# An attention and MoE kernel: the low parts of the second pair's K and V are made a step later, and four pieces of bias rows go through another pool

## Chip, cores and metric

The kernel runs on one core of a Trainium2 chip. The metric is device time of one execution in microseconds (us); lower is better. A kernel is timed in several executions, and the median is quoted.

## What is computed

The first half is attention over 4 batches, 8 heads, 576 positions and 64 features, with a bias on the scores that a small network makes from the positions. The second half takes each token's 512 attention outputs through two weight matrices with a squared ReLU between them.

```python
scores = (1.0 / np.sqrt(D)) * np.matmul(q, k.transpose(0, 1, 3, 2))
rel = pos[:, None] - pos[None, :]
x = (np.log1p(np.abs(rel)) / np.log1p(np.maximum(pos[:, None], 1.0)))[..., None]
bias = np.maximum(x @ w1 + b1, 0.0) @ w2           # 32 hidden, one value a head
scores = scores + bias.transpose(2, 0, 1)[None, :, :, :]
attn = softmax(scores)                             # over the last axis
attn_out = np.matmul(attn, v)
x = attn_out.transpose(0, 2, 1, 3).reshape(B * S, H * D)    # 2304 x 512
h = np.maximum(x @ w_in, 0.0)                      # 512 -> 2048
out = (h * h) @ w_out                              # 2048 -> 512
```

Inputs and output are float32. The kernel keeps that precision with fp16 matmuls by splitting each operand into a high part (the value cast to fp16) and a low part (the value minus its high part, again fp16), and by adding up the products high x high, high x low and low x high.

## The kernel before

**Tiling.** The four batches are packed into two pairs, p = 0 and 1. The 576 query positions of a pair are cut into five chunks c: c = 0 holds the last 64 positions of both batches, c = 1 to 4 hold 128 positions of each of the two batches. A step is one chunk and one head, so a pair has 40 steps and the program 80 (t = 0 to 79). The second pair begins at step 40, and all five chunks of a pair use the same K and V of a head.

**One step.** `qk` makes the scores in PSUM (L413 to L425). `softmax_a` adds the bias rows `bt` and takes the row maximum on VectorE (L441, two instructions for a chunk of two batches, with a short one each that reads the maximum out), then ScalarE takes exp into `s` (L445, L447). `softmax_b` casts `s` to the high part of `a` on ScalarE (L129), GpSimd subtracts for the low part (L473, L474), and a DMA on SyncE's queue transposes `a` to `at` (L476). `pv` multiplies by V three steps later (LAG = 3, L506). After four heads VectorE scales the result into `x` (L518), and after eight `finish_x` splits and transposes the finished block (L535 to L546), which then waits in a queue for the second half of the program.

**MoE units.** That half is cut into units of 256 hidden columns, and about one unit runs in each step between the attention's matmuls. `g1` makes `hp` (L560), ScalarE takes the ReLU into `r` (L566), VectorE squares it (L568) and casts the high part of `g` (L133), GpSimd subtracts for its low part (L570). `g2` follows two units later and adds to the output `o` in PSUM (L583); after eight units ScalarE evicts `o` to SBUF (L590), and it is written out (L593).

**K and V of the second pair** are read, split and laid down while the first pair still runs. A load on SyncE's queue brings one head's K or V into a staging buffer `stg` (L179; three buffers). Then `KV.split` issues, in this order: the high part as a cast on GpSimd (L131), the low part on VectorE (L191 for K, L156 for V), for V a fill of one block of the low part with zeros on GpSimd (L160), and for K a copy of one corner to the tile `kz` on ScalarE (L196, two instructions). One such split is issued at the end of each step from 32 to 35, two in steps 36 to 39, one in steps 40 to 43; each is followed by the load of a later piece. The staging buffers serve the two weight matrices before.

**Bias rows.** `hgen` makes the hidden layer for a group of rows, `bias_mm` multiplies it on TensorE (L348), evicts the sums to a tile `be` (L369 on ScalarE, or VectorE) and writes that to a DRAM table `biasd` (L378), from which `bt` is read for each step (L394). `be` takes a buffer of the `r` pool, which has five and is shared with `r`, with `o` and with the casts `cv` of the weights; of the first 16 evictions every second takes one of the four buffers of the `g` pool.

**What sets the order.** The function emits the steps one by one. A scheduler then simulates the program and fixes for each engine one order of instructions, by priorities that follow the emission and are shifted for some kinds of work. On the chip each engine, and SyncE's queue too, runs its row in order: what stands behind a waiting instruction waits as well. `pinned()` and `behind()` add dependencies that only order instructions of the same engine.

Of the kernel before, what the change touches and what calls it, by code (L numbers as in the profile page):

```python
# [12 lines left out]
AF = mybir.ActivationFunctionType  # L13
ALU = mybir.AluOpType
# [6 lines left out]
QS, KS, VS = 7, 0, 9  # L21
# [24 lines left out]
NKZ = 8  # L46
# [5 lines left out]
def tile_attention_moe(  # L52
# [11 lines left out]
    nc = tc.nc  # L64
# [49 lines left out]
    kz = const.tile([128, NKZ, 2, 128], F16, name="kz")  # L114
# [5 lines left out]
    now = [0]  # L120

    def zn(key, i=None):
        v = ENG[key]
        i = now[0] // 8 if i is None else i
        return v[min(i, len(v) - 1)]

    def cast(eng, out, in_, scale=1.0):
        if eng == "A":
            nc.scalar.activation(out=out, in_=in_, func=AF.Copy, scale=scale)  # L129
        elif eng == "P":  # L130
            nc.gpsimd.tensor_scalar(out, in_, scale, 1.0, op0=ALU.mult, op1=ALU.mult)  # L131
        else:
            nc.vector.tensor_scalar(out, in_, scale, None, op0=ALU.mult)  # L133
# [9 lines left out]
    k_t, v_t, q_t, v32 = {}, {}, {}, {}  # L143
    f32c = [(0, c) for c in ORDER[0][:NF]]

    def as_f32(t):
        return t.rearrange("p a b -> p (a b)").bitcast(F32)

    def v_split(p, h, st):
        t = vp.tile([128, 2, 640], F16, tag="v", name="v")  # L150
        cast(zn("vh", p * 8 + h), t[:, 0, :], st, float(2 ** VS))
        if p == 0:
            cast("P", st, st, float(2 ** VS))
            nc.gpsimd.tensor_tensor(t[:, 1, :], st, t[:, 0, :], op=ALU.subtract)
        else:
            nc.vector.scalar_tensor_tensor(  # L156
                out=t[:, 1, :], in0=st, scalar=float(2 ** VS), in1=t[:, 0, :],
                op0=ALU.mult, op1=ALU.subtract)

        nc.gpsimd.memset(t[64:128, 1, :].rearrange("p (b j) -> p b j", b=2)[:, :, 256:320], 0.0)  # L160
        v_t[p, h] = t

    class KV:
        def __init__(self, p, h, which):
# [16 lines left out]
        def split(self):  # L181
            st = self.st
            if self.which == "k":
                n = self.p * 8 + self.h
                t = kp.tile([128, 2, S], F16, tag="k", name="k")
                st = st[:, 0:S]
                cast(zn("kh", n), t[:, 0, :], st, float(2 ** KS))
                if zn("kl", n) == "P":
                    nc.gpsimd.tensor_tensor(t[:, 1, :], st, t[:, 0, :], op=ALU.subtract)
                else:  # L190
                    nc.vector.scalar_tensor_tensor(  # L191
                        out=t[:, 1, :], in0=st, scalar=float(2 ** KS), in1=t[:, 0, :],
                        op0=ALU.mult, op1=ALU.subtract)
                for b in range(2):
                    r = slice(64 * b, 64 * b + 64)
                    nc.scalar.activation(out=kz[r, n % NKZ, :, r], in_=t[r, :, 512 - 512 * b:576 - 512 * b], func=AF.Copy)  # L196
                k_t[self.p, self.h] = t
            elif self.p:
                v_split(self.p, self.h, st[:, 0:640])
# [75 lines left out]
    nbe = [0]  # L275

    def hg_z(G):
        return int(HID[groups.index(G) // 2])
# [4 lines left out]
    def dlen(G):  # L283
        return max(S - 16 * G, 16 * G + 16)
# [51 lines left out]
    def bias_mm(G, gi):  # L336
        ts_ = hg.pop(G)
        z = hg_z(G)
        D_ = dlen(G)
        F_, M_ = S - 16 * G, 16 * G + 16  # L340
        cuts = [0, D_] if D_ <= 512 else [0, 288, D_]
        for d0, d1 in zip(cuts[:-1], cuts[1:]):
            if gi < 4 and d0:
                bp = ps_o.tile([128, 512], F32, tag=f"o{gi % 2}", name="bp")
            else:
                bp = ps_h.tile([128, 512], F32, tag="h", name="bp")
            for t in range(4):
                nc.tensor.matmul(out=bp[32 * t:32 * t + 32, 0:d1 - d0],  # L348
                                 lhsT=w2s if gi < 4 or PATS[z][t] == "A" else w2n,
                                 rhs=ts_[t][:, d0:d1],  # L350
                                 start=True, stop=True, tile_position=(0, 32 * t))

            parts = [(max(d0, 1), min(d1, M_), True), (d0, min(d1, F_), False)]
            parts = [x for x in parts if x[1] > x[0]]
            runs = [parts] if d0 == 0 and sum(e - a for a, e, _ in parts) <= 512 else [[x] for x in parts]
            for run in runs:
                nbe[0] += 1
                if nbe[0] <= 16 and nbe[0] % 2:

                    be = as_f32(g_p.tile([128, 2, 512], F16, tag="g", name="be"))  # L360
                else:
                    be = r_p.tile([128, 512], F32, tag="r", name="be")
                p0 = 0
                for a, e, rev in run:
                    o = be[:, p0:p0 + e - a]
                    o = o[:, ::-1] if rev else o
                    p0 += e - a
                    if (zn("er" if rev else "ev") == "A") if gi > 4 else nbe[0] % 2:
                        nc.scalar.activation(out=o, in_=bp[:, a - d0:e - d0], func=AF.Identity, bias=hcst[:, z:z + 1],  # L369
                                             scale=1.0 if gi < 4 else rows_s[:, G:G + 1])  # L370
                    elif gi < 4:
                        nc.vector.tensor_scalar(o, bp[:, a - d0:e - d0], hcst[:, z:z + 1], None, op0=ALU.add)
                    else:
                        nc.vector.tensor_scalar(o, bp[:, a - d0:e - d0], rows_s[:, G:G + 1], hcst[:, z:z + 1],
                                                op0=ALU.mult, op1=ALU.add)
                a, e, rev = run[0]
                c0 = S - e if rev else S - 1 + a
                nc.sync.dma_start(out=biasd[128 * G:128 * G + 128, c0:c0 + p0], in_=be[:, 0:p0])  # L378
# [19 lines left out]

    st_ = {}
    sums = {}  # L400

    def qk(p, c, h):
        kt = k_t[p, h]
# [25 lines left out]
    def softmax_a(p, c, h):  # L429
        bt = b_t.pop((p, c, h))  # L430
        s = s_p.tile([128, 1152], F32, tag="w", name="s")
        mx = sml.tile([128, 2], F32, tag="mx", name="mx")
        nm = sml.tile([128, 2], F32, tag="nm", name="nm")
        if h == 0:
            sums[p, c] = sml.tile([128, H, 2], F32, tag="sum", name="sum")
        su = sums[p, c]
        nb = 1 if c == 0 else 2
        inv = float(2.0 ** -(QS + KS + 3))
        for b in range(nb):
            sb = b if c else h % 2  # L440
            nc.vector.tensor_tensor_reduce(  # L441
                s[:, 576 * b:576 * b + 576],
                sc[:, 960 * sb:960 * sb + 576], bt, inv, -3.0e38, ALU.add, ALU.max, mx[:, b:b + 1])
        for b in range(nb):
            nc.scalar.activation(out=nm[:, b:b + 1], in_=mx[:, b:b + 1], func=AF.Identity, scale=-1.0, bias=esc)  # L445
            sl = s[:, 576 * b:576 * b + 576]
            nc.scalar.activation(out=sl, in_=sl, func=AF.Exp, bias=nm[:, b:b + 1], accum_out=su[:, h, b:b + 1])  # L447
        st_[p, c, h] = s

    def softmax_b(p, c, h):  # L450
# [194 lines left out]
    def ld_dma(q):  # L645
        if q:
            t = q.popleft()
            t.dma()
            pend.append(t)
# [25 lines left out]
    def w_tasks(i):  # L675
        for _ in range(W_AT[i] if i < len(W_AT) else 0):
            ld_split()
            ld_dma(ws)
# [43 lines left out]
            pin[i.engine] = i.name  # L722

    @contextmanager
    def behind():
        cur = nc.cur_bb
        n0 = len(cur.bb.instructions)
        yield
        for i in cur.bb.instructions[n0:]:
            if i.engine in pin:  # L730
                tc.add_manual_dep(i, pin[i.engine], mybir.DependencyInfo(
                    mybir.DependencyClass.NoSync, mybir.DependencyReason.DATA), reason="behind")

    pin = {}
    with pinned():
# [27 lines left out]
        hgen(groups[gi])  # L763
        for h in range(2):
            bias_ld(*steps[h])
    with behind():
        kv_load(0, "v")
        ld_dma(ws)
        kv_load(2, "k")
        q_next()  # L770
        kv_load(1, "v")
        with later(200):
            ld_split()
            ld_dma(ws)
            ld_dma(ws)
            q_next()
    for t in range(NS + LAG):
        now[0] = t
        fence = ExitStack()
        if t < 2:  # L780
            fence.enter_context(behind())
        last = t - LAG
        if t < NS:
            p, c, h = steps[t]
# [32 lines left out]
        with place("kd"):  # L817
            kv_dma(t + 2)
        w_tasks(t + 1)
        for _ in range(nls[t]):  # L820
            ld_split()
            ld_dma(loads2)
# [53 lines left out]
```

## Time and profile before

| | us |
|---|---|
| median of 3 timed runs | 657.12 |
| lowest and highest | 656.75, 660.38 |
| profiled execution | 661.45 |
| its span, first to last instruction | 659.70 |
| TensorE busy in it | 615.1 |
| VectorE, ScalarE, GpSimd busy | 407.1, 388.1, 376.5 |
| mean granted clock of TensorE | 0.965 |

The profile is one execution, and its times are counted from the start of the span. Busy time of a matmul counts what the engine spends on it at the clock of the moment; the granted clock is 1.00 at full speed. A gap of an engine is put down to what released it last.

### The profile page before, as it was taken

Reading aid. Unit: us, or ns where it says so; the run is one execution under the profiler, and the core shown is the slowest. Engines: PE = TensorE matmul, PEld = TensorE weight load, DVE = VectorE, ACT = ScalarE, POOL = GpSimd, SP = SyncE. Lnnn points to the kernel's source line nnn. Section 1 sums busy time; section 2 is a strip of 40 time slices with the busy share of each in tenths; the row PEclk is TensorE's granted clock in tenths of the full one; section 3 lists DMA queues with packets and bytes.
Section 4 is the critical chain, followed back from the end, with each engine's and each line's share of the span. In section 5 each row is a group of like instructions: output and inputs, shape, how many; then the busy total and the mean of one; then the engine's idle time right before and its main releaser. Section 6 shows DMA issues by size and latency. Waiting matters only on the chain.

```text
span 659.7 us, 15574 instructions
## 1 busy us (share of the span) xinstructions
PE 615.1 (93%) x6056; PEld 394.8 (60%) x6056; DVE 407.1 (62%) x813; ACT 388.1 (59%) x856; POOL 376.5 (57%) x394
## 2 busy tenths in 40 slices
PE   5565798999899999999899999999999999999997
PEld 2223356766455566666576676676676676767664
DVE  7997999888864765585856447346545642632321
ACT  5587978788776476656656655656465564342111
POOL 2757578899665456756775465555464663432221
PEclk9698967999999999999899999999999999999999
DMA  7999888477876787889978778679787777524000
GB/s 237 278 294 319 268 255 248 155 209 178 197 173 152 162 193 176 179 180 226 221 170 158 167 134 174 140 169 153 139 172 134 154 149 155 122 56 86 17 34 16
DMA packets 206568, 112.16 MB, mean 170 GB/s; under 512 B 167072, under 2 KB 183456, under 8 KB 206496
## 3 DMA queue, kind: packets, MB, share of 16 engines
q1 hardware_dynamic: 206496, 111.19, 72.0%
q8 instruction: 47, 0.77, 0.5%
q14 instruction: 25, 0.20, 0.1%
HBM read 55.44 MB, written 15.61 MB: 108 GB/s over the span
## 4 chain that ended last, share of the span: by engine, by line
PE 69%; DVE 5%; DMA 4%; issue 2%; ACT 1%; POOL 1%; DVEq 0%; POOLq 0%; ACTq 0%
PE o L583 26%; PE hp L560 26%; PE pv L506 8%; PE sc L425 5%; PE bp L348 2%; DMA at<-a 2%; DVE hg L309 1%; PE sc L419 1%; PE sc L413 1%; DMA xt<-xh 1%; DMA stg<-vd 1%; DVE s L441 1%; DVE cv L226 0%; DVE ci L224 0%; ACT a L129 0%
## 5 line engine op out<-in xcount | busy, mean ns | idle before, releaser
L560 PE MATMUL hp<-xt,winH 128*128 128x256 f16 (+1 forms) x1280 | 195.9, 263 | 0.0
L583 PE MATMUL o<-woutH,g 128*128 128x512 f16 x576 | 185.6, 382 | 4.0 <-ACT o L590 2.2
L560 PE MATMUL hp<-xt,winL 128*128 128x256 f16 (+1 forms) x640 | 162.8, 263 | 0.0
L583 PEld LDWEIGHTS <-g 128*128 128x128 f16 x864 | 82.8, 98 | 97.0 <-issue 11.5
L560 PEld LDWEIGHTS <-winH 128*128 128x128 f16 x1280 | 117.0, 99 | 30.0 <-issue 13.6
L441 DVE CUSTOM_DVE_ANT_0 s<-sc,bt 128x576 f32<-128x576 f32 x144 | 103.5, 751 | 44.1 <-PE sc L425 34.2
L474 POOL TENSOR_TENSOR a<-s,a 128x1024 f16<-128x1024 f32 (+1 forms) x64 | 130.3, 2036 | 0.0
L568 DVE TENSOR_TENSOR r<-hp,r 128x512 f32<-128x512 f32 (+1 forms) x80 | 50.6, 632 | 118.7 <-ACT r L566 118.6
L570 POOL TENSOR_TENSOR g<-r,g 128x512 f16<-128x512 f32 (+1 forms) x80 | 86.7, 1084 | 59.1 <-DVE g L133 48.4
L447 ACT ACTIVATE s<-s,nm 128x576 f32<-128x576 f32 x144 | 111.3, 773 | 6.4
L583 PE MATMUL o<-woutL,g 128*128 128x512 f16 x288 | 109.8, 381 | 0.0
L473 POOL TENSOR_TENSOR a<-s,a 128x128 f16<-128x128 f32 (+1 forms) x64 | 28.1, 440 | 140.4 <-ACT a L129 135.5
L445 ACT ACTIVATE nm<-mx,esc 128x1 f32<-128x1 f32 x144 | 40.9, 288 | 110.8 <-DVE mx L441 110.5
L506 PE MATMUL pv<-v,at 128*128 128x64 f16 (+5 forms) x2112 | 97.9, 207 | 0.5 <-ACT at L460 0.5
L129 ACT ACTIVATE a<-s 128x1152 f16<-128x1152 f32 (+1 forms) x64 | 70.5, 1102 | 44.6 <-DMA at<-a 43.6
L566 ACT ACTIVATE r<-hp 128x512 f32<-128x512 f32 (+1 forms) x80 | 43.1, 539 | 49.6 <-PE hp L560 49.6
L506 PEld LDWEIGHTS <-at 128*128 128x128 f16 (+1 forms) x1792 | 58.3, 100 | 20.2 <-issue 8.6
L560 PEld LDWEIGHTS <-winL 128*128 128x128 f16 x640 | 62.9, 98 | 5.8
L309 DVE TENSOR_SCALAR hg<-tab_t 128x464 f32<-128x464 f32 (+17 forms) x86 | 58.9, 729 | 11.5 <-PE bp L348 11.4
L425 PE MATMUL sc<-k,q 64*128 64x512 f16 x384 | 55.6, 387 | 0.0
L369 ACT ACTIVATE be<-bp,hcst,rows_s 128x288 f32<-128x288 f32 (+29 forms) x67 | 35.8, 571 | 16.5 <-PE bp L348 11.1
L348 PE MATMUL bp<-hg,w2s 128*32 128x288 f32 (+15 forms) x152 | 36.1, 546 | 6.1 <-ACT hg L303 2.4
(88 smaller groups left out, 688.7 us busy)
## 6 DMA issues: line engine op xcount, KB each, us to landing
bt<-biasd SPq DMA_DIRECT2D x64, 288.0 KB, 3.3
stg<-w_in SPq DMA_DIRECT2D x16, 512.0 KB, 5.1
stg<-w_out SPq DMA_DIRECT2D x16, 512.0 KB, 4.7
bt<-biasd SPq DMA_DIRECT2D x32, 144.0 KB, 3.4
qst<-qd SPq DMA_DIRECT2D x32, 128.0 KB, 3.5
out<-o SPq DMA_DIRECT2D x16, 256.0 KB, 2.4
v<-vd SPq DMA_DIRECT2D x8, 320.0 KB, 4.9
stg<-vd SPq DMA_DIRECT2D x8, 320.0 KB, 4.3
```

What stands on the lines that cost most here:

```text
L129: nc.scalar.activation(out=out, in_=in_, func=AF.Copy, scale=scale)
L309: nc.vector.tensor_scalar(ht, src, scl[:, n:n + 1], None, op0=ALU.min)
L348: nc.tensor.matmul(out=bp[32 * t:32 * t + 32, 0:d1 - d0], lhsT=w2s if gi < 4 or PATS[z][t] == "A" else w2n, rhs=ts_[t][:, d0:d1], start=Tr ...
L425: nc.tensor.matmul(out=sc[:, 1024 * b:1024 * b + 512], lhsT=qt[r, qz, qs], rhs=kt[r, z, 64 * b:64 * b + 512], start=(n == 0), stop=(n == 2 ...
L441: nc.vector.tensor_tensor_reduce(s[:, 576 * b:576 * b + 576], sc[:, 960 * sb:960 * sb + 576], bt, inv, -3.0e38, ALU.add, ALU.max, mx[:, b: ...
L447: nc.scalar.activation(out=sl, in_=sl, func=AF.Exp, bias=nm[:, b:b + 1], accum_out=su[:, h, b:b + 1])
L474: nc.gpsimd.tensor_tensor(av[:, :, 640:1152], ev[:, :, 0:512], av[:, :, 0:512], op=ALU.subtract)
L506: nc.tensor.matmul(out=dst, lhsT=lhsT, rhs=vt[r, 5 * b + blk, :] if f32 else vt[:, vz, 5 * b + blk, :], start=(n == 0), stop=(n == nt - 1) ...
L560: nc.tensor.matmul(out=hp[:, f * T:f * T + T].rearrange("p (b t) -> p b t", b=nb), lhsT=wt[:, k, c0:c0 + 128], rhs=xt[:, 0:nb, z * 4 + k, ...
L568: nc.vector.tensor_tensor(rr, hp[:, 0:2 * T], rr, op=ALU.mult)
L570: nc.gpsimd.tensor_tensor(g[:, 1, 0:2 * T], r[:, 0:2 * T], g[:, 0, 0:2 * T], op=ALU.subtract)
L583: nc.tensor.matmul(out=blk["o"][b], lhsT=g[:, z, c0:c0 + 128], rhs=wt[:, 2 * u + f, :], start=(u == 0 and f == 0 and z == 0 and wt is wout ...
```

## The change

In the second pair the low part of a piece is no longer issued with its high part. It goes into a list, `lo_due`, and is issued at the end of the next step, with the fill of zeros for V, and with a dependency that only orders it behind the last softmax instruction of its engine (`soft`). The copies to `kz` are issued two steps after the split, in the same way. Nothing else of the splits changes: not the engines, the number of instructions, the buffers or the loads, though a staging buffer is in use until its low part is done. Besides, the bias rows that `bias_mm` evicts in steps 4 and 5 (four pieces, 383, 208, 143 and 448 columns) take their tile `be` from the `g` pool, where before every second of the first 16 pieces went to the `r` pool, and all that follow.

```diff
         else:
-            nc.vector.scalar_tensor_tensor(
-                out=t[:, 1, :], in0=st, scalar=float(2 ** VS), in1=t[:, 0, :],
-                op0=ALU.mult, op1=ALU.subtract)
+            lo_due.append((now[0] + 1, t, st, VS))
+            v_t[p, h] = t
+            return
...
+    def low_part(t, st, e):
+        nc.vector.scalar_tensor_tensor(
+            out=t[:, 1, :], in0=st, scalar=float(2 ** e), in1=t[:, 0, :],
+            op0=ALU.mult, op1=ALU.subtract)
+        if e == VS:
+            nc.gpsimd.memset(t[64:128, 1, :].rearrange("p (b j) -> p b j", b=2)[:, :, 256:320], 0.0)
...
+                    lo_due.append((now[0] + 1, t, st, KS))
+                if self.p:
+                    kz_due.append((now[0] + 2, n, t))
+                else:
+                    kz_copy(n, t)
...
-                if nbe[0] <= 16 and nbe[0] % 2:
+                if (nbe[0] <= 16 and nbe[0] % 2) or 4 <= now[0] < 6:
...
+            soft[i.ins.engine] = i.ins.name
...
         w_tasks(t + 1)
+        while lo_due and lo_due[0][0] <= t:
+            with behind(soft):
+                low_part(*lo_due.popleft()[1:])
+        while kz_due and kz_due[0][0] <= t:
+            with behind(soft):
+                kz_copy(*kz_due.popleft()[1:])
         for _ in range(nls[t]):
             ld_split()
             ld_dma(loads2)
```

On VectorE, at the end of step 37 and in step 38, the program stood like this before; names carry buffer numbers, `v_4534` and `k_4414` are the two pieces that GpSimd casts in the same step, and L441 is the softmax of the step.

```order
L156 SCALAR_TENSOR_TENSOR v_4421<-stg_4297,v_4421 128x640
L191 SCALAR_TENSOR_TENSOR k_4286<-stg_4181,k_4286 128x576
L568 TENSOR_TENSOR r_4240<-hp_4215,r_4240 128x512
L133 TENSOR_SCALAR g_4241<-r_4240 128x512
L441 ISA s_4308,mx_4309<-sc_141,bt_4097 128x576
L441 ISA mx_4309 128x1
L441 ISA s_4308,mx_4309<-sc_141,bt_4097 128x576
L441 ISA mx_4309 128x1
L156 SCALAR_TENSOR_TENSOR v_4534<-stg_4425,v_4534 128x640
L191 SCALAR_TENSOR_TENSOR k_4414<-stg_4291,k_4414 128x576
L568 TENSOR_TENSOR r_4356<-hp_4331,r_4356 128x512
L133 TENSOR_SCALAR g_4357<-r_4356 128x512
```

Now the same stretch reads as follows; `k_4284` and `v_4288` were cast a step earlier than the softmax above them.

```order
L166 SCALAR_TENSOR_TENSOR v_4178<-stg_4072,v_4178 128x640
L586 TENSOR_TENSOR r_4233<-hp_4208,r_4233 128x512
L133 TENSOR_SCALAR g_4234<-r_4233 128x512
L457 ISA s_4301,mx_4302<-sc_141,bt_4092 128x576
L457 ISA mx_4302 128x1
L457 ISA s_4301,mx_4302<-sc_141,bt_4092 128x576
L457 ISA mx_4302 128x1
L166 SCALAR_TENSOR_TENSOR k_4284<-stg_4176,k_4284 128x576
L166 SCALAR_TENSOR_TENSOR v_4288<-stg_4180,v_4288 128x640
L586 TENSOR_TENSOR r_4349<-hp_4324,r_4349 128x512
L133 TENSOR_SCALAR g_4350<-r_4349 128x512
```

The low parts that stood behind this softmax, of the pieces cast in the same step, have made room for those of pieces cast a step before.

On ScalarE, at the end of step 38, before:

```order
L447 ACTIVATE s,sum<-s,nm 128x576
L566 ACTIVATE r<-hp 128x512
L129 ACTIVATE a<-s 128x2x576
L196 ACTIVATE kz<-k 64x2x64 x2
L590 ACTIVATE o<-o_3586,os 128x512
L590 ACTIVATE o<-o_3587,os 128x512
```

The same place now:

```order
L464 ACTIVATE s,sum<-s,nm 128x576
L177 ACTIVATE kz<-k 64x2x64 x2
L584 ACTIVATE r<-hp 128x512
L129 ACTIVATE a<-s 128x2x576
L608 ACTIVATE o<-o_3586,os 128x512
L608 ACTIVATE o<-o_3587,os 128x512
```

The copy to `kz` has moved from between the cast `a` and the two evictions of `o` to directly behind exp, and it copies an earlier head.

On ScalarE in steps 4 and 5, before:

```order
L307 ACTIVATE hg<-tab_t 128x448 x2
L129 ACTIVATE winH<-cv 128x2x256
L196 ACTIVATE kz<-k 64x2x64 x2
L445 ACTIVATE nm<-mx,esc 128x1
L447 ACTIVATE s,sum<-s,nm 128x576
L369 ACTIVATE be<-bp,hcst,rows_s 128x383
L129 ACTIVATE woutH<-cv 128x512
L369 ACTIVATE be<-bp,hcst,rows_s 128x208
```

And now:

```order
L322 ACTIVATE hg<-tab_t 128x448 x2
L384 ACTIVATE be<-bp,hcst,rows_s 128x383
L384 ACTIVATE be<-bp,hcst,rows_s 128x208
L129 ACTIVATE winH<-cv 128x2x256
L177 ACTIVATE kz<-k 64x2x64 x2
L462 ACTIVATE nm<-mx,esc 128x1
L464 ACTIVATE s,sum<-s,nm 128x576
L129 ACTIVATE woutH<-cv 128x512
```

The two evictions of the bias rows have moved ahead of a weight cast and of the softmax.

## Rows read from the trace of the kernel before

**Rows 1.** The page: busy time of the engines, and TensorE's clock in 40 slices.

```profile
PE 615.1 (93%) x6056; PEld 394.8 (60%) x6056; DVE 407.1 (62%) x813; ACT 388.1 (59%) x856; POOL 376.5 (57%) x394
...
PEclk9698967999999999999899999999999999999999
```

**Rows 2.** Busy time by stretches of one step each; columns in the head.

```profile
core 0: us, PE busy (x) PEld busy (x) DVE busy (x) ACT busy (x) POOL busy (x), PEclk, DMA share, GB/s
...
303.64:310.70 7.06, 7.06 (x80) 4.71 (x76) 4.32 (x8) 3.25 (x8) 3.85 (x6) 1.00 0.93 216
310.70:321.79 11.09, 8.90 (x79) 5.15 (x76) 8.42 (x12) 6.89 (x16) 9.79 (x12) 0.85 0.86 192
...
400.00:407.06 7.06, 7.06 (x74) 4.88 (x74) 6.48 (x12) 4.06 (x9) 6.01 (x5) 1.00 0.58 146
```

**Rows 3.** TensorE's instructions in time: start, duration, what, in brackets idle before.

```profile
314.24 0.27 PE L560 MATMUL hp<-xt,winL 128*128 128x256 f16 x1
...
316.70 0.38 PE L583 MATMUL o<-woutH,g 128*128 128x512 f16 x1 [2.19 <-ACT o L590]
```

**Rows 4.** The chain that ended last: two groups of o matmuls, start and us.

```profile
316.70 4.44 PE o L583 x12
...
325.60 2.59 PE o L583 x12
```

**Rows 5.** The chain of waits into the gap, stretch 270 to 320 us.

```profile
307.67 1.17 ACT a L129
...
312.61 0.70 POOL v L131
...
313.37 1.16 issue
314.53 0.76 DVE k L191
...
315.96 0.69 ACT o L590
```

**Rows 6.** ScalarE's instructions in time, around the gap.

```profile
313.13 1.16 ACT L129 ACTIVATE a<-s 128x1152 f16<-128x1152 f32 x1 [0.98 <-DMA at<-a]
315.31 0.63 ACT L196 ACTIVATE kz<-k 64x128 f16<-64x128 f16 x2 [1.02 <-DVE k L191]
```

**Rows 7.** VectorE's instructions in time, steps 38 and 39.

```profile
304.97 1.28 DVE L156 SCALAR_TENSOR_TENSOR v<-stg,v 128x640 f16<-128x640 f32 x1 [3.16 <-POOL v L131]
306.17 0.74 DVE L191 SCALAR_TENSOR_TENSOR k<-stg,k 128x576 f16<-128x576 f32 x1
...
307.54 0.43 DVE L133 TENSOR_SCALAR g<-r 128x512 f16<-128x512 f32 x1
307.89 0.75 DVE L441 CUSTOM_DVE_ANT_0 s<-sc,bt 128x576 f32<-128x576 f32 x1
...
315.91 2.01 DVE L133 TENSOR_SCALAR g<-r 128x512 f16<-128x512 f32 x1
```

**Rows 8.** SyncE's queue in time: a V load and the transposition behind it.

```profile
306.94 0.33 SPq L179 DMA_DIRECT2D stg<-vd  x1
307.37 3.90 SPq L476 DMA_TRANSPOSE at<-a  x1
```

**Rows 9.** GpSimd's instructions in time, step 38.

```profile
301.73 0.43 POOL L473 TENSOR_TENSOR a<-s,a 128x128 f16<-128x128 f32 x1
302.11 2.13 POOL L474 TENSOR_TENSOR a<-s,a 128x1024 f16<-128x1024 f32 x1
304.21 0.72 POOL L131 TENSOR_SCALAR v<-stg 128x640 f16<-128x640 f32 x1
```

**Rows 10.** The staging tile, 270 to 345 us: from issue to landing.

```profile
DMA to landing us min/median/max: 2.8/3.7/5.2
```

**Rows 11.** VectorE's instructions in time, step 3: its long wait there.

```profile
58.12 0.69 DVE L226 SCALAR_TENSOR_TENSOR cv<-stg,ci 128x512 uint32<-128x512 uint32 x1 [3.08 <-DMA biasd<-be]
```

**Rows 12.** Busy time from 100 to 120 us; columns as in rows 2.

```profile
100.00:120.00 20.00, 17.87 (x121) 13.21 (x121) 17.61 (x32) 16.25 (x40) 16.82 (x21) 0.74 0.71 217
```

More of the change, by code (lines that the diff above doesn't have):

```diff
@@ L155, in v_split, with kz_copy @@
         else:
-            nc.vector.scalar_tensor_tensor(
-                out=t[:, 1, :], in0=st, scalar=float(2 ** VS), in1=t[:, 0, :],
-                op0=ALU.mult, op1=ALU.subtract)
+            lo_due.append((now[0] + 1, t, st, VS))
+            v_t[p, h] = t
+            return
         nc.gpsimd.memset(t[64:128, 1, :].rearrange("p (b j) -> p b j", b=2)[:, :, 256:320], 0.0)
         v_t[p, h] = t
+    lo_due = deque()
+    def low_part(t, st, e):
[4 more added lines that the diff above has]
+            nc.gpsimd.memset(t[64:128, 1, :].rearrange("p (b j) -> p b j", b=2)[:, :, 256:320], 0.0)
+    kz_due = deque()
+    def kz_copy(n, t):
+        for b in range(2):
+            r = slice(64 * b, 64 * b + 64)
+            nc.scalar.activation(out=kz[r, n % NKZ, :, r], in_=t[r, :, 512 - 512 * b:576 - 512 * b], func=AF.Copy)
     class KV:
@@ L190, in split @@
                 else:
[L191 to L196, printed above, removed]
+                    lo_due.append((now[0] + 1, t, st, KS))
[3 more added lines that the diff above has]
+                    kz_copy(n, t)
                 k_t[self.p, self.h] = t
@@ L400, in tile_attention_moe @@
     sums = {}
+    soft = {}
     def qk(p, c, h):
@@ L440, in softmax_a @@
             sb = b if c else h % 2
-            nc.vector.tensor_tensor_reduce(
+            i = nc.vector.tensor_tensor_reduce(
                 s[:, 576 * b:576 * b + 576],
                 sc[:, 960 * sb:960 * sb + 576], bt, inv, -3.0e38, ALU.add, ALU.max, mx[:, b:b + 1])
+            soft[i.ins.engine] = i.ins.name
         for b in range(nb):
@@ L446, in softmax_a @@
             sl = s[:, 576 * b:576 * b + 576]
-            nc.scalar.activation(out=sl, in_=sl, func=AF.Exp, bias=nm[:, b:b + 1], accum_out=su[:, h, b:b + 1])
+            i = nc.scalar.activation(out=sl, in_=sl, func=AF.Exp, bias=nm[:, b:b + 1], accum_out=su[:, h, b:b + 1])
+            soft[i.ins.engine] = i.ins.name
         st_[p, c, h] = s
@@ L724, in behind @@
     @contextmanager
-    def behind():
+    def behind(last):
         cur = nc.cur_bb
@@ L729, in behind @@
         for i in cur.bb.instructions[n0:]:
-            if i.engine in pin:
-                tc.add_manual_dep(i, pin[i.engine], mybir.DependencyInfo(
+            if i.engine in last:
+                tc.add_manual_dep(i, last[i.engine], mybir.DependencyInfo(
                     mybir.DependencyClass.NoSync, mybir.DependencyReason.DATA), reason="behind")
@@ L765, in tile_attention_moe @@
             bias_ld(*steps[h])
-    with behind():
+    with behind(pin):
         kv_load(0, "v")
@@ L780, in tile_attention_moe @@
         if t < 2:
-            fence.enter_context(behind())
+            fence.enter_context(behind(pin))
         last = t - LAG
```

## Prediction

> **What bounds the kernel now.** I read the page first, then busy time by stretches of one step, then TensorE's own instructions around the one step that is long, and last the chain of waits that leads into it. TensorE is busy 93% of the span, and its clock line shows full speed from about 125 us to the end but for one slice near 310 us [rows 1]. From about 175 us on every step of the attention loop has the same length: between two score blocks lie 7.06 us, in which TensorE has no gap, in the stage of the change (303.64 to 310.70) as well as long behind it (400 us) [rows 2]. So a wait of another engine there costs nothing until TensorE itself stops. It stops once: the step from 310.70 to 321.79 takes 11.09 us with TensorE busy 8.90 and a mean granted clock of 0.85 [rows 2]. That is 4.03 us over 7.06, and two pieces make it up. TensorE's hp matmuls end at 314.51, and the next o matmul starts 2.19 us later, released by ScalarE's eviction of the last block's output [rows 3]. Behind that gap the granted clock falls to the lower of its two levels (1.2 GHz), and the twelve o matmuls take 4.44 us where the same twelve take 2.59 one step later [rows 4]: 1.85 us. The sum, 4.04, is the step's excess.
>
> Why the eviction is late is told by the chain [rows 5]. ScalarE's cast a (1.17 us from 307.67) lets GpSimd's subtract a and its g go, and then the cast of V's high part at 312.61; only then can VectorE do V's low part (in the chain the 1.16 under issue from 313.37), then K's low part (0.76), then ScalarE the kz copy, and behind that, in ScalarE's order, the eviction (0.69). ScalarE sat 1.02 us before the kz copy for VectorE's k [rows 6].
>
> **The change, part by part.** Profiled, the program takes 661.45 us: 659.70 of span and 1.75 around it. The median of the three timed runs is 657.12, 4.33 less.
>
> *Low parts a step later.* Nothing is added or taken out: 16 low parts, 8 zero fills and 16 kz copies stay, in another place. What goes is VectorE's wait for GpSimd. In step 38 V's low part stood 3.16 us for the cast of V, and the softmax row max, whose scores were finished long before, came only at 307.89, behind both low parts [rows 7]. With the low parts of a piece that was cast a step before, placed behind the softmax, the max runs some 3 us earlier, at about 304.7. ScalarE's part of step 38 follows it: the kz copy waits for nothing fresh any more, stands ahead of r and a, and the eviction comes directly behind a. Even if a stayed at 313.13, where it is now (0.98 us of that is a wait for the transposition of step 36 [rows 6]), the eviction would end at 313.13 + 1.16 + 0.69 = 314.98, 0.47 us behind the 314.51 at which TensorE wants it. And a moves earlier too: the SyncE queue stood until 306.94 at a V load that waited for VectorE's low parts, and only then, at 307.37, issued the transposition of step 36, whose input GpSimd had finished at 304.24 [rows 8, 9]. So the stall is bounded between 0 and 0.47 us where it was 2.19; I take 0. Without the gap the clock has no reason shown here to fall, and the 1.85 goes as well. In the profiled execution this part is worth 4.03 us.
>
> What is late next? A staging buffer is now held a step longer, and there are three. From step 36 on, with two splits a step, a V load has to wait for a low part that itself stands behind a softmax, and GpSimd's cast of that V stands ahead of the subtract a of the same step. Queued behind such a wait are the transposition, its pv three steps later, and the softmax two steps later, which takes the same s buffer (two of them). The loop over two steps is: softmax 2 x 0.75, K's low part 0.74, V's low part 1.28 [rows 7], issue 0.33 [rows 8], landing 3.7 [rows 10], cast 0.72, a 0.43 + 2.13 [rows 9]: 10.83 us. Two steps of TensorE last 14.12, so 3.29 us cover it, and 1.79 with the slowest landing of 5.2 [rows 10]. The last V is finished in step 44 and first read in step 50; K of head 7 in step 41 and read in step 47. These I cost at nothing, with the loop as the cover.
>
> The low parts' new place is beside the subtract a. VectorE and GpSimd hinder each other there: the cast g that took VectorE 0.43 us in step 38 took 2.01 in step 39, beside a subtract like the one of 2.13, and V's low part, beside the cast of K, took 1.28 for 640 columns where K's took 0.74 for 576 [rows 7, 9]. So a low part costs between nothing and 2.13 more there, and the loop at most 12.96, its cover at least 1.16; the sum stays, and the upper bound goes into the second rival. The Trainium skill, "SBUF — State Buffer", section "Who interferes with whom", speaks against the move: a VectorE instruction with two SBUF inputs and a GpSimd instruction that reads SBUF shut each other out for a whole instruction, whoever comes second. By that rule the upper bound would be met whenever GpSimd comes first, and I would give the second rival 0.14 in place of 0.10; the durations of steps 38 and 39 agree with it as far as they go.
>
> *Four pieces of bias rows in g buffers.* The evictions 383 and 208 (step 4) and 143 and 448 (step 5) no longer wait for an r buffer. The first two move ahead of a weight cast and of a softmax on ScalarE, their writes on the SyncE queue go ahead of a weight load, and the weight casts of these steps get their r buffers two places sooner. VectorE, though, is what this stage runs on: its long wait there, 3.08 us at 58.12, is for a buffer with bias rows to be written out, of step 2 [rows 11], which the change doesn't touch, and from 100 to 120 us VectorE is busy 17.61 of 20 [rows 12]. The g buffers are free until the MoE starts, past 110 us. I cost this part at 0, with bounds from the clock there: from 100 to 120 us the granted clock is 0.74, so (1 - 0.74) / 0.5 = 0.52 of the stretch at the lower level [rows 12], and a different order of TensorE's work can move that. At best VectorE's 2.39 idle us there (20 - 17.61) go; at worst a half-speed stretch of that size (20 x 0.52 = 10.4 us, so 5.2 us of work) falls where TensorE alone sets the pace.
>
> **The timed runs.** The stall belongs to one profiled execution, 4.33 us above the median. The runs shown lie at 656.75, 657.12 and 660.38, so a loss of 3 to 4 us seems to be in some executions and not in others. What the median run pays of the 4.03 is not shown: between 0 and 4.03. I take the wait alone, 2.19, without the clock step that followed it: 657.12 - 2.19 = 654.9.
>
> **The rivals.**
> - *The median run pays all of it*: the excess step is the same in every execution, and the rest of the 4.33 is the profiling. Then 657.12 - 4.03 = 653.1. For it: the chain is made of waits, not of chance. Against it: the runs' spread.
> - *Slower, by the staging buffers*: a V load issued behind a transposition on SyncE (3.90 us [rows 8]) and landing in 5.2 makes the loop 10.83 + 3.90 + 1.50 = 16.23, or 2.11 over 14.12 (it decides from 3.29 us of delay); steps 37 to 40 hold two such loops, and with the low part held for 2.13 more each costs 4.24, together 8.5 less the eviction's gain: 657.12 + 8.5 - 2.19 = 663.4. Against it: in the new order the load that matters stands behind a bias load, and the transposition ahead of it has its input by then.
> - *No change*: the median run has no stall, the gain is in the profile alone: 657.1.
> - *The clock in the front part*: 654.9 - 2.4 = 652.5 or 654.9 + 5.2 = 660.1.
>
> **How the numbers follow.** Forecast 654.9: 0.41 (its own range 653.5 to 656.3). All of it, 653.1: 0.23. No change, 657.1: 0.18. Slower by the loads, 663.4 (anything from 659 up): 0.10. Clock, both ways: 0.04 each. A measurement of this kernel can tell about 0.5%, 3.3 us, from no change. Below 653.8 fall 0.19 of the second case, 0.11 of the forecast's lower end and 0.04 of the clock: 0.34. Above 660.4 fall 0.08 of the slower case and 0.02 of the clock: 0.10. The rest, 0.56, is the same within 0.5%. The range leaves out the upper part of the slower case and the lowest tenth: 651.8 to 660.0.
>
> **What would show it.** Right: no TensorE gap and no low clock between 300 and 330 us, all steps from 34 to 50 at 7.06 us, the eviction directly behind a, no VectorE wait for a V cast, and a profiled time near 657.4. Wrong: a wait of GpSimd for a V load and a late pv in steps 40 to 43 (second rival); the same steps without a gap but an unchanged median (third); a half-clock stretch elsewhere than before 116 us (fourth).

## The result, and the profile after

The changed kernel takes 664.37 us (median of 8 runs, 660.75 to 667.45) against 656.94 us before (8 runs beside it, 655.98 to 660.38): a ratio of 1.0102, 95% interval 1.0077 to 1.0128. Timed once more in another session, 663.79 us stand against 658.48 us, 1.0072 (1.0049 to 1.0094). It is slower by 0.7 to 1.0%, where 654.9 us and at most 660.0 us had been forecast. The ratios here and below are estimates over the executions and differ a little from the quotient of the two medians.

The first profile of the changed kernel is, of all its runs, the fastest (660.75 us), so it must be read beside the others. TensorE's share and its clock line answer to [rows 1]:

```profile
PE 613.5 (93%) x6056; PEld 395.1 (60%) x6056; DVE 409.4 (62%) x813; ACT 387.4 (59%) x856; POOL 382.3 (58%) x394
...
PEclk9598957899999999999999999999999999999999
```

The half-clock slice near 310 us is gone in this execution, and GpSimd is busy 382.3 us for the same 394 instructions, 5.8 us more than in [rows 1]. Busy time by steps around the place of [rows 2], from one score block to the next:

```profile
303.80:310.86 7.06, 7.06 (x80) 4.73 (x76) 3.98 (x8) 4.74 (x11) 3.77 (x7) 1.00 1.15 193
317.90:325.40 7.50, 7.22 (x80) 4.79 (x77) 3.19 (x9) 2.38 (x5) 6.97 (x8) 1.00 0.69 202
...
332.40:340.10 7.70, 5.02 (x72) 3.80 (x69) 6.04 (x11) 4.76 (x12) 7.56 (x8) 1.00 1.08 213
```

The step of 11.09 us in [rows 2] has gone, but three steps later, at 332.40, TensorE is busy 5.02 of 7.70 us. In time order, TensorE there (start, duration, idle before in brackets):

```profile
332.71 0.82 PE L441 MATMUL sc<-k,q 64*128 64x512 f16 x6
336.21 0.99 PE L524 MATMUL pv<-v,at 128*128 128x64 f16 x28 [2.68 <-DMA at<-a]
```

What the change was to do at the old place it does. ScalarE's two evictions now follow the cast a directly, where in [rows 6] the copy to kz stood between:

```profile
312.12 1.16 ACT L129 ACTIVATE a<-s 128x1152 f16<-128x1152 f32 x1 [2.56 <-DMA at<-a]
...
313.19 1.25 ACT L608 ACTIVATE o<-o,os 128x512 f32<-128x512 f32 x2
```

The gap has not vanished, it has changed its cause: a pv that waits 2.68 us for its transposition. The chain of waits that ends in it (start, us, what):

```profile
321.56 0.59 POOL q L131
...
322.17 0.69 DVE q L283
...
323.95 0.70 DVE s L457
...
325.34 1.58 DVE k L166
326.92 1.70 DVE v L166
...
329.11 7.06 DMA at<-a
...
336.21 0.99 PE pv L524 x28
```

GpSimd's cast of q is late; VectorE's low part of q waits for it; the softmax stands behind that, and behind the softmax, as the change has it, the two low parts. They take 1.58 and 1.70 us where [rows 7] have 0.74 and 1.28. On SyncE's queue, whose loads and transpositions are issued in this order, everything stands behind the two loads of the next q. They come at 322.89, just when VectorE's low part of q is done (322.17 + 0.69), and the queue waited for that:

```profile
322.89 1.29 SPq L276 DMA_DIRECT2D qst<-qd  x2
324.28 3.16 SPq L494 DMA_TRANSPOSE at<-a  x1
327.53 0.52 SPq L409 DMA_DIRECT2D bt<-biasd  x1
328.16 0.85 SPq L195 DMA_DIRECT2D stg<-vd  x2
329.11 5.14 SPq L494 DMA_TRANSPOSE at<-a  x1
```

The second of the two V loads needs the staging buffer that the low part of V frees. That wait is short here: its turn comes at 328.53, the low part ends at 328.62. The late start of the queue is the larger part, and it goes back to GpSimd's cast of q. The landing of 7.06 us is long, but it alone makes no late pv: in the runs below with ScalarE's zeros and with the maximum, which have no loss, the transposition of this step lands after 7.7 and 7.6 us. Why GpSimd is late its own instructions tell:

```profile
309.40 0.73 POOL L131 TENSOR_SCALAR v<-stg 128x640 f16<-128x640 f32 x1 [3.23 <-DMA stg<-vd]
...
310.48 2.72 POOL L492 TENSOR_TENSOR a<-s,a 128x1024 f16<-128x1024 f32 x1
...
315.47 1.27 POOL L131 TENSOR_SCALAR v<-stg 128x640 f16<-128x640 f32 x1
...
317.10 2.71 POOL L492 TENSOR_TENSOR a<-s,a 128x1024 f16<-128x1024 f32 x1
...
321.52 0.62 POOL L131 TENSOR_SCALAR q<-qst 128x512 f16<-128x512 f32 x1
```

It waits 3.23 us for a V load, and then runs without a break to the cast of q with subtracts of 2.71 us and a cast of 1.27 us, where [rows 9] have 2.13 and 0.72.

### The profile page after: what moved, and what is told of

Its sections match the earlier page's. It is cut to its first block, busy times and chain, and to the rows that moved or that the text cites. A ratio compares the mean times of both kernels' runs of the same rounds, so it can differ in the third digit from the quotient of the medians.

```text
span 659.0 us, 15565 instructions
## 1 busy us (share of the span) xinstructions
PE 613.5 (93%) x6056; PEld 395.1 (60%) x6056; DVE 409.4 (62%) x813; ACT 387.4 (59%) x856; POOL 382.3 (58%) x394
## 4 chain that ended last, share of the span: by engine, by line
PE 59%; DMA 6%; POOL 5%; DVE 4%; issue 4%; ACT 3%; SPq 1%; POOLq 0%; DVEq 0%; ACTq 0%
PE hp L578 22%; PE o L601 22%; PE pv L524 6%; DMA at<-a 4%; PE sc L441 4%; POOL a L492 2%; PE bp L363 2%; DMA xt<-xh 1%; POOL g L588 1%; DVE hg L324 1%; DVE s L457 1%; ACT a L129 1%; PE sc L429 1%; PE sc L435 1%; DMA stg<-vd 1%
## 5 line engine op out<-in xcount | busy, mean ns | idle before, releaser
L492 POOL TENSOR_TENSOR a<-s,a 128x1024 f16<-128x1024 f32 (+1 forms) x64 | 132.8, 2076 | 0.0
L441 PE MATMUL sc<-k,q 64*128 64x512 f16 x384 | 55.0, 387 | 0.0
```

The source lines that it names most:

```text
L441: nc.tensor.matmul(out=sc[:, 1024 * b:1024 * b + 512], lhsT=qt[r, qz, qs], rhs=kt[r, z, 64 * b:64 * b + 512], start=(n == 0), stop=(n == 2 ...
L492: nc.gpsimd.tensor_tensor(av[:, :, 640:1152], ev[:, :, 0:512], av[:, :, 0:512], op=ALU.subtract)
```

## Experiments

Each experiment was timed beside the kernel before on the same chip. The numbers: median, median of before beside it, ratio with its 95% interval.

**Low parts alone, bias rows alone, and the change again.** The first takes the changed kernel and puts the old rule for `be` back, the second takes the kernel before and puts in the new one:

```diff
-                if (nbe[0] <= 16 and nbe[0] % 2) or 4 <= now[0] < 6:
+                if nbe[0] <= 16 and nbe[0] % 2:
```

> Only the low parts and kz copies are moved; the bias rows take their buffers as before. Theory A (the V loads, held up by low parts that stand behind a softmax, make a late transposition and a late pv in steps 36 to 42): as slow as the whole change, about 664 us, and the late pv is in its trace. Theory B (the bias pieces reorder the front part and the half-clock stretches there last longer): about 655 to 657 us, like before or a little faster.

> Only the four pieces of bias rows go to the g buffers; the low parts stay with the high parts. Theory A: about 657 us, as before, with the gap in front of the o matmuls near 314 us. Theory B: about 664 us, with more half-clock time or more idle TensorE before 180 us than the kernel before.

> The changed kernel once more, for a second execution in profile: its first profile was the fastest of eight runs. Theory A: between 320 and 345 us a pv that waits for its transposition, longer than the 2.7 us of the first profile or with a half-clock stretch behind it. Theory B: that place as in the first profile, and the loss before 180 us.

| | us | before | ratio |
|---|---|---|---|
| low parts alone | 661.57 | 658.48 | 1.0047 (1.0030 to 1.0065) |
| bias rows alone | 660.51 | 658.48 | 1.0037 (1.0015 to 1.0059) |
| the change again | 663.79 | 658.48 | 1.0072 (1.0049 to 1.0094) |

Neither theory alone holds: each gave the whole loss, 664 us, to its own part. Both parts cost, 3.1 and 2.0 us, and 5.1 is what the two make together, against 5.3 for the whole. The granted clock does not set the runs apart on the average: each run lists its span and mean clock, and (1 - clock) x 2 x span, the time at the lower level, averages 48.2 us over 21 runs of before, 48.7 with the low parts alone, 45.0 with the bias rows alone and 49.7 with both, each mean with a standard error of 1 to 3 us.

With the low parts alone the program up to the step where the splits begin is in the same order as before on every engine, so its 3.1 us are made behind it. Its profile has the late pv, longer, and at the lower clock (1.67 us for the 28 matmuls that took 0.99 above):

```profile
335.18 1.67 PE L524 MATMUL pv<-v,at 128*128 128x64 f16 x28 [3.43 <-DMA at<-a]
```

There the V load does wait for its staging buffer, 0.7 us. In the second profile of the whole change the late pv waits 2.32 us, less than in the first, and its 28 matmuls take 1.24 us.

**Where the bias rows cost.** With the bias rows alone the order behind step 23 is that of before, so the 2.0 us are made in front. Four executions have the new order of the front part, nine the old one. From the softmax of step 16 to that of step 24 the old order takes 60.9 to 61.7 us in all nine, the new one 63.7 to 64.4 in all four; up to step 16, which holds the moved pieces, no difference stands out of the spread. Busy time by that stretch, before and with the low parts alone:

```profile
141.48:202.38 60.90, 58.17 (x616) 35.23 (x617) 46.66 (x90) 47.48 (x103) 46.30 (x48) 1.00 0.72 174
```

```profile
140.20:201.10 60.90, 58.16 (x615) 35.22 (x616) 44.81 (x91) 47.47 (x103) 46.71 (x48) 1.00 0.75 175
```

And with the whole change:

```profile
138.62:202.52 63.90, 58.77 (x624) 36.46 (x627) 46.22 (x90) 47.83 (x103) 45.88 (x49) 1.00 0.73 167
```

TensorE's idle time there is 2.73 us before (60.90 - 58.17) and 5.13 with the change, at full clock in both. What it waits for in the stretch (engine and operation, what it waits for, us, times, longest), before:

```profile
PE o L583 <- POOL g L570: 1.8, 2, 1.2
PE bp L348 <- ACT be L369: 0.9, 1, 0.9
```

With the change:

```profile
PE hp L578 <- DVE r L586: 1.7, 1, 1.7
PE sc L435 <- DVE mx L457: 1.3, 2, 0.7
PE bp L363 <- ACT be L384: 1.1, 1, 1.1
PE bp L363 <- ACT hg L322: 0.5, 1, 0.5
PE hp L578 <- DMA xt<-xh: 0.4, 1, 0.4
```

These are other waits: hp and the scores wait for VectorE. With the bias rows alone the four evictions lie 3.5 to 4.4 us earlier than before (61.5, 62.1, 68.5 and 68.8 us in place of 65.5, 66.5, 72.0 and 72.4), and the two traces show TensorE's work in another order in some twenty places from there up to 190 us. The last of them lie where TensorE is busy 58 of 61 us.

**Only step 5, only step 4.** The kernel before with the g buffers for the pieces of one step:

```diff
-                if nbe[0] <= 16 and nbe[0] % 2:
+                if (nbe[0] <= 16 and nbe[0] % 2) or 5 <= now[0] < 6:
```

(and 4 <= now[0] < 5 for the other.)

> The kernel before, with only the pieces of step 5 in the g buffers. TensorE's order behind 150 us is that of the run with steps 4 and 5 but for a few rows. Theory B1 (the loss of the bias part lies in the new order of TensorE's work between 150 and 180 us, where hp waits 1.8 us for VectorE's square): as with both steps, 660 us, and idle time of about 4.7 us there in place of 2.7. Theory B2 (it lies in the evictions themselves, in proportion to their number): about half, 658.7 us.

> The kernel before, with only the pieces of step 4 in the g buffers. The order that follows is another one than with steps 4 and 5. Theory B1: the time follows TensorE's idle time between 150 and 180 us in this order, not the number of pieces, and so may fall on either side of 657.6. Theory B2: about half the loss, 658.7 us, as with step 5 alone.

Step 5 alone: 660.74 against 657.38 us, 1.0045 (1.0021 to 1.0069). Step 4 alone: 669.12 us, 1.0170 (1.0142 to 1.0199). The cost is not in proportion to the pieces: two of them alone cost 3.4 us or 11.7, where the four together cost 2.0. (3.4 and 2.0 lie within each other's intervals; 11.7 does not.) Step 5 alone has nearly the order of both, and the same stretch:

```profile
138.10:201.80 63.70, 58.79 (x624) 36.38 (x626) 45.92 (x90) 47.86 (x103) 45.37 (x49) 1.00 0.75 167
```

4.91 us idle. With step 4 alone it is 64.90 us with 59.48 busy, 5.42 idle:

```profile
142.30:207.20 64.90, 59.48 (x593) 34.77 (x593) 48.82 (x86) 47.08 (x102) 45.20 (x48) 0.97 0.71 163
```

That is 2.7 us more than before, of its 11.7. Work has also moved behind the stretch: of the hp matmuls 192 lie in it against 212 before, and 119 against 96 in the next one, which takes 41.90 us (to 249.10) where it took 36.25 (to 238.63), TensorE busy all the time in both. What made the rest is open. That a new order costs in this stretch is shown by all these profiles; which of the places does it is open too.

**The kernel before again.**

> The kernel before once more, for a second profile. Theory P (its usual execution has no gap in the stage of the second pair's K and V, the first profile was an unlucky one): about 657 us and steps of 7.06 us through 300 to 330 us, or a shorter gap there without the half-clock stretch. Theory Q (the gap is in every execution): the gap of 2 us before the o matmuls and a half-clock stretch behind it, whatever the total.

659.29 us, one run. The gap is a quarter of that in [rows 3], and no half-clock stretch follows:

```profile
315.01 0.27 PE L560 MATMUL hp<-xt,winL 128*128 128x256 f16 x1
315.83 0.38 PE L583 MATMUL o<-woutH,g 128*128 128x512 f16 x1 [0.55 <-ACT o L590]
```

Five profiles in all have the old order of this stage. The gap is 2.19 and 2.01 us in two, 0.55 and 0.49 in two others, and the run with only step 4 has none. The gap is shorter here from both ends: the eviction starts at 315.10 us, 0.86 earlier than in [rows 5], and TensorE comes to it 0.77 later (315.28 against 314.51). For the eviction one link differs: the transposition that SyncE issues at 299.95 us in [rows 8]'s execution, one step ahead of the one shown there, and at 300.02 in this one. ScalarE's cast a, which waits for it, starts at 305.93 here after 1.83 us of waiting, and at 307.67 in [rows 5]:

```profile
305.93 1.16 ACT L129 ACTIVATE a<-s 128x1152 f16<-128x1152 f32 x1 [1.83 <-DMA at<-a]
...
315.10 1.27 ACT L590 ACTIVATE o<-o,os 128x512 f32<-128x512 f32 x2
```

Of the transpositions around it the slowest landed after 7.6 and 7.8 us in the executions with the long gap, 5.8 and 5.9 in those with the short one (6.6 in the one without). So theory Q does not hold: the long gap on which the forecast rested is in some executions and not in others. What the median run pays of it these profiles do not tell.

**The kz copies alone.** The low parts are issued with the high parts as before, and the bias rows are as before; the copies stay two steps later:

```diff
-            lo_due.append((now[0] + 1, t, st, VS))
+            low_part(t, st, VS)
...
-                    lo_due.append((now[0] + 1, t, st, KS))
+                    low_part(t, st, KS)
```

> The kernel before with only the kz copies moved two steps later and behind the softmax; the low parts stay with the high parts. Theory T1 (the delayed low parts hold the staging buffers, so V loads and casts come late) and theory T2 (delayed low parts on VectorE run beside GpSimd's subtracts and lengthen both): no loss, 655 to 659 us against 658.5, and the eviction of o no longer waits for K's low part, so no gap before the o matmuls or one under 1 us. Theory T3 (the place of the kz copies is what costs): about 661.5 us as with low parts and copies moved.

659.58 against 657.65 us, 1.0019 (1.0003 to 1.0034): a small loss and no gain, above the range of theories T1 and T2 and below the time of T3. Its interval overlaps that of the low parts alone. What makes it is open: its profile has two short gaps, a wait of o for the eviction of 0.8 us and one of a score block for VectorE of 0.5, and the kernel before has between none and 2.2 us there. Of the runs below that move the copies in the same way, three have no loss that can be told.

```profile
PE o L601 <- ACT o L608: 0.8, 1, 0.8
PE sc L435 <- DVE mx L457: 0.5, 1, 0.5
```

**One split a step.** With the low parts moved (bias rows as before), and with the kernel before:

```diff
-    nls = [0] * 32 + [1] * 4 + [2] * 4 + [1] * 4 + [0] * 50
+    nls = [0] * 32 + [1] * 16 + [0] * 50
```

> Low parts and kz copies moved as in the change (bias rows as before), but one split a step in steps 32 to 47 in place of one, two, one in steps 32 to 43. Theory T1: the V loads no longer wait long for a staging buffer, the late pv near 332 us is gone, about 657 to 659 us. Theory T2: the pairs on VectorE and GpSimd are as many as before, the subtracts of 2.7 us stay, and so does most of the loss: about 661 us.

> The kernel before, with one split a step in steps 32 to 47 and nothing else. With half the rate no engine has two splits beside one subtract in a step: the gap before the o matmuls should go, 655 to 658 us if the usual execution pays for it (theory Q), 658.5 unchanged if it does not (theory P).

With the low parts moved: 658.34 against 657.65 us, 1.0007 (0.9990 to 1.0023); the kernel before: 657.50 us, 1.0001 (0.9977 to 1.0026). The second does not price the old gap, since its profile still has one of 0.6 us before the o matmuls. At half the rate the moved low parts cost nothing that can be told, and TensorE's wait for a transposition is 0.2 us. But this does not speak for the staging buffers alone: GpSimd still waits 12.3 us for V loads here, against 7.5 with the low parts alone, and the longest subtract is 2.31 us, not 2.71. The rate changes both.

**Staging buffers or VectorE beside GpSimd.** Two runs take the low parts moved (bias rows as before) and take one of the two away. In the first ScalarE writes zeros in the low part's place, reading the staging buffer; in the second VectorE's instruction keeps its size and both operands in SBUF, but reads a constant table, so that the buffer is free after GpSimd's cast:

```diff
-        nc.vector.scalar_tensor_tensor(
-            out=t[:, 1, :], in0=st, scalar=float(2 ** e), in1=t[:, 0, :],
-            op0=ALU.mult, op1=ALU.subtract)
+        nc.scalar.activation(out=t[:, 1, :], in_=st, func=AF.Copy, scale=0.0)
```

```diff
+        n = 640 if e == VS else S
         nc.vector.scalar_tensor_tensor(
-            out=t[:, 1, :], in0=st, scalar=float(2 ** e), in1=t[:, 0, :],
+            out=t[:, 1, :], in0=tab_t[:, 0:n], scalar=float(2 ** e), in1=t[:, 0, :],
```

> Low parts and kz copies moved as in the change (bias rows as before), but the moved instruction is a plain write of zeros by ScalarE that reads the staging buffer, so the low parts of the second pair's K and V are left out. The staging buffer is held as long as with the change; VectorE has no two-operand instruction beside GpSimd's subtracts any more. Theory T1 (staging buffers alone): the late pv near 332 us stays, about 661 us. Theory T2 (VectorE and GpSimd hinder each other): the subtracts fall back from 2.7 to 2.1 us, no late pv, 656 to 658.5 us.

> Low parts and kz copies moved as in the change (bias rows as before), but the low part takes its float32 operand from a constant table and not from the staging buffer, so it is not the low part, and the staging buffer is free as soon as GpSimd has cast the piece. VectorE's work, its operands and its place are those of the change. Theory T1: GpSimd's waits for V loads go, no late pv, 656 to 658.5 us. Theory T2: subtracts of 2.7 us and the late pv stay, about 661 us. If both are needed, each of this and the run on ScalarE recovers most of the loss.

ScalarE's zeros: 656.23 against 657.38 us, 0.9986 (0.9972 to 0.9999). The whole loss is gone though the buffers are held as with the change and GpSimd waits 10.0 us for V loads. Its cast of q starts 0.5 us before the scores of its step (317.99 against 318.47), where with the change it starts 3.6 us behind them (321.52 against 317.90), and its subtracts take 2.13 us again:

```profile
306.56 2.13 POOL L490 TENSOR_TENSOR a<-s,a 128x1024 f16<-128x1024 f32 x1
```

Buffers free early: 659.70 us, 1.0035 (1.0020 to 1.0051). A loss stays, 2.3 us (659.70 - 657.38) in place of 3.1; the intervals overlap, so the share of the buffers in the time is not resolved. GpSimd has no wait for a V load in this stage, but its subtracts are long, and TensorE has two gaps, the old one, 1.3 us, and the new one, 0.8 in place of 3.4. So the held buffers have a part in the late pv:

```profile
307.52 2.71 POOL L493 TENSOR_TENSOR a<-s,a 128x1024 f16<-128x1024 f32 x1
```

```profile
PE o L602 <- ACT o L609: 1.3, 1, 1.3
PE pv L525 <- DMA at<-a: 0.8, 1, 0.8
```

**The same VectorE time with one operand.** The run with ScalarE's zeros still left open that VectorE simply had less to do. So VectorE got a maximum over the staging buffer in the low part's place, with its result unused:

```diff
         nc.scalar.activation(out=t[:, 1, :], in_=st, func=AF.Copy, scale=0.0)
+        dm = sml.tile([128, 2], F32, tag="dm", name="dm")
+        nc.vector.tensor_reduce(dm[:, 0:1], st, axis=AX.X, op=ALU.max, apply_absolute_value=True)
```

> As the run with ScalarE's zeros (the low parts of the second pair's K and V are left out), but in the low part's place VectorE reads the staging buffer with a maximum over its columns: as much time of VectorE, one operand from SBUF in place of two, the result unused. Theory T2 (two operands beside GpSimd's subtracts are what costs): still no late pv and no lengthened subtracts, 656 to 658.5 us. Theory T4 (VectorE's time behind the softmax is what costs, whatever its operands): the loss returns, 659.5 to 661 us.

656.11 against 658.58 us, 0.9965 (0.9939 to 0.9991). No loss, and in the profile TensorE waits for nothing in that stage. The groups of the sixteen VectorE instructions (busy time, mean ns) and GpSimd's subtract beside them:

```profile
L168 DVE TENSOR_REDUCE dm<-stg 128x1 f32<-128x640 f32 x8 | 6.5, 810 | 0.0
L168 DVE TENSOR_REDUCE dm<-stg 128x1 f32<-128x576 f32 x8 | 6.0, 747 | 0.0
```

```profile
303.99 2.13 POOL L492 TENSOR_TENSOR a<-s,a 128x1024 f16<-128x1024 f32 x1
```

With the low parts moved, the same two groups have means of 1057 and 1133 ns (undisturbed, a low part takes 0.81 and 0.75 us):

```profile
L166 DVE SCALAR_TENSOR_TENSOR k<-stg,k 128x576 f16<-128x576 f32 x8 | 9.1, 1133 | 0.0
L166 DVE SCALAR_TENSOR_TENSOR v<-stg,v 128x640 f16<-128x640 f32 x7 | 7.4, 1057 | 2.3 <-POOL v L131 2.3
```

So theory T2 holds against T1 and T4: neither the held buffers alone nor VectorE's time costs, but the low part, which reads two operands from SBUF, beside GpSimd's subtract. Which of the two is lengthened follows from which began first. In the profile of the change the low part of V that begins before a subtract keeps its 1.04 us, and the subtract takes 2.71; the low part of K that begins inside a subtract takes 1.66, and the subtract keeps its 2.13. The softmax instruction inside that subtract takes the 0.75 us that it takes elsewhere:

```profile
316.78 1.04 DVE L166 SCALAR_TENSOR_TENSOR v<-stg,v 128x640 f16<-128x640 f32 x1 [0.62 <-POOL v L131]
317.10 2.71 POOL L492 TENSOR_TENSOR a<-s,a 128x1024 f16<-128x1024 f32 x1
...
324.17 2.13 POOL L492 TENSOR_TENSOR a<-s,a 128x1024 f16<-128x1024 f32 x1
324.58 0.75 DVE L457 CUSTOM_DVE_ANT_0 s<-sc,bt 128x576 f32<-128x576 f32 x1
325.26 1.66 DVE L166 SCALAR_TENSOR_TENSOR k<-stg,k 128x576 f16<-128x576 f32 x1
```

The maximum writes only one column, and so by itself does not separate the second operand from the written output. The softmax does: it writes 576 columns to SBUF but has one operand there (`bt`; `sc` is in PSUM), and it keeps its 0.75 us inside the subtract. One operand is no safeguard for every instruction, though. A cast with one operand in SBUF is held up as well: the cast g in [rows 7] took 2.01 us, and in the run with the maximum a cast of q took 2.03 us beside a subtract:

```profile
L133 DVE TENSOR_SCALAR q<-qst 128x512 f16<-128x512 f32 x1 | 2.0, 2027 | 0.0
```

The runs with ScalarE's zeros and with the maximum are even a little faster than the kernel before, by 0.9 us (0.1 to 1.8) and 2.3 us (0.6 to 4.0). Neither has a gap before the o matmuls, and both leave the low parts out.

## Why the prediction was wrong

*What bounds the kernel* was read rightly: TensorE from about 175 us on, so that only its own gaps count. The old gap's cause, the chain in [rows 5], was right too, and the moved copies let the eviction follow a.

*The worth of the gap* was taken as 2.19 us in the median run, from one execution. It rested on less than it seemed: of five executions with the old order of this stage two have the long gap, two have about 0.5 us and one has none. What it is worth in the median run stays open; the two runs without gap and loss were faster by 0.9 and 2.3 us. Even at 0 this term would bring the time to 657.1 and not to 664.4, so it is not what failed most.

*"These I cost at nothing, with the loop as the cover"* is the step that turned the sign. The loop was worked out with durations from before, and the 3.29 us of cover were set against late loads; the longer low parts were admitted as a bound, the longer subtracts and casts of GpSimd not at all. A V load for which GpSimd waits 3.23 us, subtracts of 2.71 and a cast of 1.27 used up the cover: the cast of q came 3.6 us behind the scores of its step, the SyncE queue behind it, and a pv 2.68 us late. The moved low parts and copies, forecast to gain 2.19 us, cost 3.1. The second rival had the place (a wait of GpSimd for a V load, then a late pv in steps 40 to 43) and the sign, with 8.5 us for a cost of 3.1, but its cause, a V load that waits for its staging buffer, is not enough: with the buffers held and no low part on VectorE the loss is gone, and with the buffers free early the late pv shrinks to 0.8 us but most of the loss seems to stay. It was given 0.10.

*The rule weighed there was the better guide.* The subtract took 2.71 us behind a low part against 2.13 otherwise, the low parts up to 2.34, and a maximum of the same length with one operand cost nothing. That is what the Trainium skill, "SBUF — State Buffer", section "Who interferes with whom", says: two SBUF inputs on VectorE contend with a GpSimd instruction that reads SBUF, and `tensor_reduce` never contends. The prediction would have moved a chance by 0.04 for it, and left it at 0.10, since the sum had "cover". It also took the cast g of 2.01 us for a case of this rule; that cast has one input in SBUF, so the sentence on two inputs does not cover it.

*The four bias pieces* were costed at 0 with VectorE as the limit of that stage, and bounds from the clock. They cost 2.0 us alone, the second step that failed. Up to step 16 no loss shows; the term that was missing is the order that the scheduler makes of everything behind the evictions. The difference of the orders could be seen beforehand: TensorE's work is placed otherwise up to step 23, past the 175 us from which the prediction itself counts every gap. It was read for steps 4 and 5 only.

*The clock in the front part* was a rival with 0.08. The half-speed time is the same on the average within its scatter, so neither of its two times came. Where pv ran at the lower clock (1.67 us), that followed its wait.

*What would show it* was named rightly: the late pv and GpSimd's wait for a V load are there, the eviction is directly behind a.

## What to carry to other kernels

When VectorE work is moved to end a wait, look at what GpSimd does at the new place: a low part with two SBUF operands and a GpSimd subtract delay each other, the one that comes second being held up, and a cover worked out from undisturbed durations is too large. A gap in one profiled execution is worth what the other executions pay, so profile twice before a gain is booked. And where a scheduler sets the order, compare the order of the bounding engine to its last difference, not only around the edit: a buffer changed in steps 4 and 5 cost its time between steps 16 and 24.

## What the runs showed of the hardware that was not expected

The landing time of a transposition issued at the same moment of the same program was 5.8 us in one execution and 7.6 in another; by way of the cast a, that is about half of the difference between a gap of 0.55 and one of 2.19 us. The hindrance between VectorE and GpSimd goes both ways: GpSimd's subtract grew by 0.58 us (2.71 against 2.13), its cast of V by 0.55 (1.27 against 0.72), and VectorE's low part of K from 0.75 to as much as 2.34. The softmax on VectorE, with one operand in SBUF and one in PSUM, took 0.75 us inside a subtract as elsewhere.
